# Sorted block attention and a residual MLP on one core: crossbar turns for q, moved mixing slots, and a last tile in halves

## Chip, cores and metric

The kernel runs on one core of a Trainium2 chip. The metric is the device time in microseconds. The page gives the granted TensorE clock as 0.999 of full speed.

## The reference

Shapes: q, k and v are (4 batches, 8 heads, 768 rows, 64), sort_net is (4, 8, 8, 8), and the output is (4, 768, 512), all float32. The MLP has 512 channels and 2048 hidden units.

```python
P = sort_net                       # five rounds of exp, divided by row sums, then column sums
for _ in range(5):
    P = exp(P - max(P)); P = P / sum(P, -1); P = P / sum(P, -2)
k_sorted = einsum('bhij,bhjcd->bhicd', P, k_b)      # 8 blocks of 96 rows are mixed
v_sorted = einsum('bhij,bhjcd->bhicd', P, v_b)
attn = softmax(q_b @ k_sb.T / sqrt(64))             # block by block
x = attn @ v_sb                                     # then heads side by side: (4, 768, 512)
a1 = alpha1 * x + beta1
tok = einsum('ts,bsd->btd', w_tok, a1)              # the token layer
u = x + lam * tok
a2 = alpha2 * u + beta2
out = u + lam * (max(a2 @ w_ch1, 0) @ w_ch2)        # the channel layers
```

## The kernel before

**The skeleton.** The channel layers of the four batches are the frame on which everything else hangs. A batch b is done in two halves hf of 384 rows. For each half, `h_unit` (line 692) makes 16 tiles of the hidden layer: four matmuls of 384 columns each into a PSUM tile h_ps, then a ReLU on ScalarE into hTa or hTb. Then `ch_unit` (line 695) makes three output tiles of 128 rows, each as four parts of four matmuls of 512 columns with hT as the stationary operand. VectorE multiplies the output tile by lam, and GpSimd adds u (VectorE in the last half of the last batch). Two DMAs of SP, of 96 and 32 rows, write it out.

I write h(b,hf) and c(b,hf) for these two stages. A stage h has the places h0 to h15 and a stage c the places c0 to c11, each of them a point behind one tile or part. `put(b, hf, kind, n, ...)` (line 791) hangs other work on a place, and the main loop at the end (lines 859 to 868) runs it there. This is an order written out by hand. TensorE, VectorE, ScalarE and GpSimd keep it as written, since they are recorded through a class `Engine` (line 55; so nearly every operation has line 65 in the profile). DMAs that SP issues are not recorded through it. SP takes them one after the other in the order that the builder gives them.

**What hangs on the frame.** While batch p = b - 1 goes through its channel layers, batch b is prepared:

- `load_kv` and `load_q` (lines 191 and 184) are loads by GpSimd's DMA queue from float32 to f16. q arrives as qn, with rows on the partitions, in six DMAs. The next batch is asked for at c11 of c(p,0).
- `mix_matrix` (354) makes the mixing matrices bigV, bigM and bigP of a batch: one matmul (repv_ps) and six VectorE operations (sel, red, bigV, bigM, two of bigP). For batches 2 and 3 it hangs at c5 of c(b - 2, 1).
- `mix_v` (508) mixes v in three parts of two matmuls (mix_ps), each copied by VectorE. `bounce_v` writes the result to DRAM with two SP DMAs (vscr), and `back_v` reads it as Vs, in another layout, with a third. For batches 2 and 3 these are at h10, h11, h12; h12; and c0.
- `mix_k` (523) mixes k in three parts of eight matmuls (kmix_ps), each copied by four operations into kT. For batches 2 and 3: c0 and c6 on ScalarE, c3 on VectorE.
- `q_turn_late` (495) turns q: for each of four head pairs six transposes on TensorE into a PSUM tile qt_ps, and one copy into qT by VectorE or ScalarE. For batches 2 and 3: c1, c4, c7, c7.
- `score` (397) needs all of kT and qT. It makes eight scores of a batch; each is eight matmuls (sc_ps) and one exp (et). `pv` (460) multiplies by Vs (x_ps). VectorE then takes a reciprocal and a product (x) and, one pv later, two operations for a. For batches 2 and 3, the scores start at c8 and pv at c10 of c(p,0), and they go on through h(p,1). `tails` moves some rows of a and x with six copies by VectorE.
- `moe_tok` (650) is the token layer: 18 matmuls for three row tiles (tok_ps), then on VectorE toktmp and u in f16 for each tile, and u in float32 on GpSimd. `moe_cross` (660) turns the f16 u by three crossbar DMAs of SP (uT), and `moe_affine` (667) makes a2T, on which the next h stage works. For the first half of batch 1 tokens and turns are at c5 and a2T at c8 of c(0,1); for batches 2 and 3 they are at c3 and c7.

**Buffers.** PSUM tiles come from two pools: psA with two slots (scores, x, mix, kmix, repv) and psB with four, which go round (h, ch, tok, qt). The output tile ost has two buffers, qT and qn one each, kT two.

Of the kernel before, what the change touches and what calls it, by code (L numbers as in the profile page):

```python
# [7 lines left out]
FT = mybir.dt.float32  # L8
F16 = mybir.dt.float16
# [7 lines left out]
def kernel(  # L17
# [20 lines left out]
    nc = tc.nc  # L38
# [315 lines left out]
    def mix_matrix(b):  # L354
        mix_values(b, psa)
        big = att.tile([128, 2, H * NB], F16, name="bigM", tag="bigM", bufs=3)
        dve.tensor_tensor(
            big[:], bigV[b][:].rearrange("p h i -> p (h i)").unsqueeze(1).to_broadcast([128, 2, H * NB]),
            mth[:].unsqueeze(2).to_broadcast([128, 2, H * NB]), ALU.mult,
        )  # L360
        bigM[b] = big
        bgp = att.tile([128, 2, 2, H4, NB], F16, name="bigP", tag="bigP", bufs=3)
        for th in range(2):
            dve.tensor_tensor(
                bgp[:, :, th, :, :], bigV[b][:].rearrange("p (g a) i -> p a g i", a=2),
                mth[:, th:th + 1].unsqueeze(2).unsqueeze(3).to_broadcast([128, 2, H4, NB]), ALU.mult,
            )
        bigP[b] = bgp
# [121 lines left out]
    def tails(x, lo, hi, eng):  # L490
        flush()
        for a in range(3):
            eng(x[96:128, a:a + 4:3, lo:hi], x[32 * a:32 * a + 32, 6:8, lo:hi])

    def q_turn_late(b, g, eng):
        if g == 0:
            qT_of[b] = att.tile([128, H4, S], F16, name="qT", tag="qT", bufs=1)
        ps = psb([128, S], F16, "qt_ps")
        for kt in range(NT):
            pe.transpose(  # L500
                ps[:, kt * 128:(kt + 1) * 128],
                qn_of[b][:, kt, 2 * g:2 * g + 2, :].rearrange("p a d -> p (a d)"), ident16[:],
            )
        eng(qT_of[b][:, g, :], ps[:])
# [3 lines left out]
    def mix_v(b, n, eng):  # L508
        if n == 0:
            mixed[b] = att.tile([128, HB, D], F16, name="mixed", tag="mixed", bufs=1)  # L510
        ps = psa([128, 2, 512], FT, "mix_ps")
        raw = raw_of[(b, 1)][:].rearrange("p t d -> p (t d)")
        for m in range(2):
            pe.matmul(
                ps[:, m, :], bigM[b][:].rearrange("p a x -> p (a x)"),
                raw[:, n * 1024 + m * 512:n * 1024 + (m + 1) * 512], start=True, stop=True,
            )
        eng(
            mixed[b][:, n * 16:(n + 1) * 16, :].rearrange("p t d -> p (t d)"),
            ps[:].rearrange("p m f -> p (m f)"),  # L520
        )

    def mix_k(b, n, engs):
        if n == 0:
            kT_of[b] = att.tile([128, H4, NB, BLK], F16, name="kT", tag="kT", bufs=2)
        ps = psa([128, 8, 128], FT, "kmix_ps")
        raw = raw_of[(b, 0)]
        for tp in range(8):
            pe.matmul(
                ps[:, tp, :], raw[:, 16 * n + 2 * tp:16 * n + 2 * tp + 2, :].rearrange("p t d -> p (t d)"),  # L530
                bigP[b][:].rearrange("p a t g i -> p (a t g i)"), start=True, stop=True,
            )
        dst = kT_of[b][:].rearrange("p g i (th tp par) -> p th (g i) tp par", th=2, par=2)
        for par in range(2):
            for h2 in range(2):
                engs[2 * par + h2](
                    dst[h2 * 64:h2 * 64 + 64, :, :, 8 * n:8 * n + 8, par],
                    ps[par * 64:par * 64 + 64, :, h2 * 64:h2 * 64 + 64].rearrange(
                        "p n (th c) -> p th c n", th=2
                    ),  # L540
                )

    def bounce_v(b):
        for th in range(2):
            nc.sync.dma_start(
                vscr[b, :, th * HB:(th + 1) * HB, :], mixed[b][th * 64:(th + 1) * 64, :, :],
            )
# [102 lines left out]
    def moe_tok(b, kt, ps):  # L650
        u32 = u_of[b]
        tok_part(b, kt, 0, C, ps)
        if b not in u16_of:
            u16_of[b] = moep.tile([128, NT, C], F16, name="u16", tag="u16", bufs=1)
        tmp = att.tile([128, C], FT, name="toktmp", tag="toktmp", bufs=2)
        dve.tensor_tensor(tmp[:], tok_of[(b, kt)][:], lamB[:], ALU.mult)
        dve.tensor_tensor(u16_of[b][:, kt, :], tmp[:], x_of[b][:, kt, :], ALU.add)
        (pool if b else dve).tensor_tensor(u32[kt], tmp[:], x_of[b][:, kt, :], ALU.add)
# [33 lines left out]
    def h_unit(b, hf, m):  # L692
        h_part(b, hf, m, range(CT))

    def ch_unit(b, hf, kk, part=(0, HT)):
        hT = hT_of[(b, hf)]
        kt = 3 * hf + kk
        if part[0] == 0:
            ch_of[0] = psb([128, C], FT, "ch_ps")
        cps = ch_of[0]  # L700
        for m in range(*part):
            pe.matmul(
                cps[:], hT[m][:, kk * 128:(kk + 1) * 128], W2p[:, m, :],
                start=(m == 0), stop=(m == HT - 1),
            )
        if part[1] < HT:
            return
        ost = att.tile([128, C], FT, name="ost", tag="ost", bufs=2)
        dve.tensor_tensor(ost[:], cps[:], lamB[:], ALU.mult)
        (dve if b == B - 1 and hf == 1 else pool).tensor_tensor(ost[:], ost[:], u_of[b][kt], ALU.add)  # L710
        act_out(out[b, kt * 96:(kt + 1) * 96, :], ost[0:96, :])
        act_out(out[b, TAIL + kt * 32:TAIL + (kt + 1) * 32, :], ost[96:128, :])
# [78 lines left out]
    def put(b, hf, kind, n, *todo):  # L791
        at.setdefault((b, hf, kind, n), []).extend(todo)
# [7 lines left out]
    for ks in range(NT):  # L800
        put(0, 0, "h", ks, lambda ks=ks: prep_wtok(ks, 1, psb, (dve.tensor_copy, act.copy)[ks % 2]))
    for n in range(1, B):
        put(max(n - 2, 0), n > 1, *(("h", 10), ("c", 5))[n > 1], lambda n=n: mix_matrix(n))
    put(0, 0, "h", 9, lambda: moe_cross(0, 1))
    for g in range(CT):
        put(0, 0, "h", g, lambda g=g: first_affine(0, slice(0, 128), slice(0, NT), slice(g * 128, (g + 1) * 128)))
# [3 lines left out]
    for b in range(1, B):  # L810
        p = b - 1
        off = 3 if b == 1 else 0
        for n in range(3):
            put(p, 0, "h", (13 if b == 1 else 10) + n, lambda b=b, n=n: mix_v(b, n, dve.tensor_copy))
        put(p, 0, "h", 15 if b == 1 else 12, lambda b=b: bounce_v(b))
        put(p, 0, "c", 4 if b == 1 else 0, lambda b=b: back_v(b))
        for n in range(3):
            put(p, 0, "c", off + 3 * n, lambda b=b, n=n: mix_k(b, n, ((act.copy, dve.tensor_copy)[n % 2],) * 4))
        for g in range(H4):
            put(p, 0, "c", off + (1, 4, 7, 7)[g], lambda b=b, g=g: q_turn_late(b, g, (dve.tensor_copy, act.copy, dve.tensor_copy, act.copy)[g]))  # L820
        if b + 1 < B:
            put(p, 0, "c", 11, lambda b=b: load_kv(b + 1), lambda b=b: load_q(b + 1))
        seq = [("s", 0), ("s", 1), ("s", 2), ("p", 0), ("s", 3), ("p", 1), ("p", 2), ("s", 4), ("p", 3), ("s", 5),
               ("p", 4), ("s", 6), ("p", 5), ("s", 7), ("p", 6), ("p", 7)]
        if b == 1:
            when = [("h", 0), ("h", 1), ("h", 2), ("h", 3), ("h", 4), ("h", 5), ("h", 6), ("h", 7), ("h", 8), ("h", 9),
                    ("h", 10), ("h", 11), ("h", 12), ("h", 13), ("h", 14), ("h", 15)]
        else:
            when = [("c", 8), ("c", 9), ("c", 10), ("c", 10), ("c", 11), ("c", 11), ("h", 0), ("h", 1), ("h", 2), ("h", 3),
                    ("h", 4), ("h", 5), ("h", 6), ("h", 8), ("h", 9), ("h", 11)]  # L830
        for (kind, n), (ph, at_) in zip(seq, when):
            f = (lambda b=b, n=n: score(b, n // 2, n % 2, psa)) if kind == "s" else (lambda b=b, n=n: pv(b, n // 2, n % 2))
            put(p, 1 if ph == "h" else 0, ph, at_, f)
        last = [("h", 12), ("h", 15)][b == 1]
        put(
            p, 1, *last, lambda b=b: tails(a1_of[b], 0, C, dve.tensor_copy),
            lambda b=b: tails(x_of[b], 0, C, dve.tensor_copy),
        )
        put(p, 1, "h", 4, lambda b=b: moe_start(b))
        for kt in range(3):  # L840
            put(p, 1, "c", 5 if b == 1 else 3, lambda b=b, kt=kt: moe_tok(b, kt, psb))
        put(p, 1, "c", 5 if b == 1 else 3, lambda b=b: moe_cross(b, 0))
        put(p, 1, "c", 8 if b == 1 else 7, lambda b=b: moe_affine(b, 0))
        for kt in range(3):
            put(b, 0, "h", 2 * kt, lambda b=b, kt=kt: moe_tok(b, 3 + kt, psb))
        put(b, 0, "h", 4, lambda b=b: moe_cross(b, 1))
        put(b, 0, "h", 13, lambda b=b: moe_affine(b, 1))
# [51 lines left out]
```

## Time and profile before

| | us |
|---|---|
| median of 7 runs | 277.2 |
| lowest, highest | 276.68, 279.44 |
| the profiled execution | 276.64 |
| its span in the trace | 274.9 |
| TensorE busy | 261.8 |
| VectorE, ScalarE, GpSimd busy | 166.5, 126.0, 97.3 |
| c(1,0) in the trace | 120.15 to 135.90 |
| h(1,1) | 135.90 to 150.10 |
| c(1,1) | 150.10 to 164.57 |
| h(2,0) | 164.57 to 180.15 |
| c(2,0) | 180.15 to 195.90 |

Times of a profile are from the start of its span. PE is TensorE, PEld its weight loads, DVE VectorE, ACT ScalarE, POOL GpSimd, SP SyncE; SPq is SP's queue of DMA issues. A row of the timeline has the start, the duration, the engine, the line, the operation with output and inputs, the number of instructions merged, and in brackets how long the engine had been idle before, with what ended that. Matmuls overlap in the pipeline, so the time from the start of one row to the start of the next is what TensorE spends; the duration of a row holds the latency of its last matmul too. A row of the table of stretches has the stretch, its length, then busy time and instruction count of PE, PEld, DVE, ACT and POOL, then the granted clock, the busy share of the DMA engines and GB/s.

### The profile page before, as it was taken

How to read it: one execution, taken by the hardware profiler on the slowest of the kernel's cores; microseconds unless marked ns; L12 is line 12 of the kernel's file. 1: busy time of each engine (PE TensorE's matmuls, PEld its weight loads, DVE VectorE, ACT ScalarE, POOL GpSimd, SP SyncE). 2: the span in 40 equal slices, each digit the busy share in tenths (PEclk: the TensorE clock that was granted, in tenths of full speed). 3: DMA queues.
4: the chain of work that ended last, by engine and by line, in shares of the span. 5: the costliest groups of instructions: out<-in, count | busy, mean ns of one | idle time of the engine just before them, and what ended most of it. 6: DMA issues, size and time to landing. Idle time of an engine off the chain costs nothing.

```text
span 274.9 us, 5418 instructions
## 1 busy us (share of the span) xinstructions
PE 261.8 (95%) x2205; PEld 141.3 (51%) x2205; DVE 166.5 (61%) x345; ACT 126.0 (46%) x231; POOL 97.3 (35%) x104
## 2 busy tenths in 40 slices
PE   7998999999999998999999999999999999999992
PEld 3466655445555444555455445555465445545540
DVE  5787517987378985466498784555679755121042
ACT  2588557225886002565777003566774004605600
POOL 8647103601571184402282556203100746032000
PEclk9999999999999999999999999999999999999999
DMA  6999999999999333249479932159300223012012
GB/s 105 215 202 191 206 208 214 176 114 185 126 180 170 24 95 97 40 99 119 89 149 182 91 86 70 38 118 127 102 4 2 76 57 79 19 38 76 2 38 76
DMA packets 60684, 29.46 MB, mean 107 GB/s; under 512 B 50082, under 2 KB 56242, under 8 KB 60660
## 3 DMA queue, kind: packets, MB, share of 16 engines
q0 software_dynamic: 26352, 15.34, 40.0%
q1 hardware_dynamic: 34308, 13.79, 26.3%
q8 instruction: 17, 0.28, 0.4%
q14 instruction: 7, 0.06, 0.1%
HBM read 32.79 MB, written 8.65 MB: 151 GB/s over the span
## 4 chain that ended last, share of the span: by engine, by line
PE 82%; DVE 8%; ACT 4%; DMA 3%; issue 2%; DVEq 0%; ACTq 0%; POOLq 0%
PE h_ps L65 29%; PE ch_ps L65 25%; PE tok_ps L65 10%; PE x_ps L65 3%; PE sc_ps L65 3%; ACT kT L65 2%; DVE x L65 2%; DVE a L65 2%; PE warm_ps L65 2%; DMA q<-in_q_dram 2%; PE kmix_ps L65 1%; PE mix_ps L65 1%; PE v_ps L65 1%; DVE ost L65 1%; PE qt_ps L65 1%
## 5 line engine op out<-in xcount | busy, mean ns | idle before, releaser
L65 PE MATMUL h_ps<-a2T,W1p 128*128 128x384 bf16 x512 | 95.9, 326 | 1.9 <-DVE a2T L65 1.5
L65 ACT ACTIVATE hTa<-h_ps 128x384 bf16<-128x384 f32 x96 | 47.0, 493 | 90.6 <-PE h_ps L65 90.4
L65 PE MATMUL ch_ps<-W2p,hTa 128*128 128x512 bf16 x288 | 68.4, 379 | 0.0
L65 POOL TENSOR_TENSOR ost<-ost,u 128x512 f32<-128x512 f32 x21 | 26.6, 1267 | 113.7 <-DVE ost L65 108.6
L65 PEld LDWEIGHTS <-W1p 128*128 128x128 bf16 x512 | 47.3, 98 | 33.5 <-issue 2.5
L65 PEld LDWEIGHTS <-hTa 128*128 128x128 bf16 x288 | 27.2, 98 | 29.0
L65 DVE TENSOR_TENSOR ost<-ch_ps,lamB 128x512 f32<-128x512 f32 x24 | 16.6, 691 | 39.7 <-PE ch_ps L65 36.8
L65 POOL TENSOR_TENSOR u<-toktmp,x 128x512 f32<-128x512 f32 x18 | 29.3, 1643 | 8.9 <-DVE toktmp L65 8.9
L65 PE MATMUL tok_ps<-a,w_tokT 128*128 128x512 f16 x126 | 29.7, 379 | 0.0
L65 ACT ACTIVATE et<-sc_ps 96x768 f16<-96x768 f32 (+1 forms) x32 | 25.6, 811 | 2.6 <-PE sc_ps L65 2.6
L65 PE MATMUL ch_ps<-W2p,hTb 128*128 128x512 bf16 x96 | 24.6, 379 | 0.0
L65 DVE TENSOR_TENSOR toktmp<-tok_ps,lamB 128x512 f32<-128x512 f32 x21 | 14.4, 688 | 13.3 <-PE tok_ps L65 12.0
L65 ACT CAST kT<-kmix_ps 64x512 f16<-64x512 f32 x24 | 17.1, 714 | 10.0 <-PE kmix_ps L65 9.7
L65 ACT ACTIVATE hTb<-h_ps 128x384 bf16<-128x384 f32 x32 | 15.7, 491 | 9.7 <-PE h_ps L65 9.5
L65 PEld LDWEIGHTS <-w_tokT 128*128 128x128 f16 x126 | 12.2, 98 | 13.8 <-DVE a L65 0.4
L65 DVE TENSOR_TENSOR u<-toktmp,x 128x512 f16<-128x512 f32 (+1 forms) x24 | 17.8, 750 | 0.7
L65 POOL DMA_DIRECT2D qn<-in_q_dram x18 | 16.0, 918 | 5.8 <-DMA raw<-in_v_dram 5.8
L65 DVE TENSOR_TENSOR x<-x_ps,rcb 96x512 f16<-96x512 f32 x24 | 16.5, 687 | 0.8
L65 PE MATMUL x_ps<-Vs,et 96*128 96x65 f16 (+4 forms) x288 | 14.4, 195 | 2.0 <-DVE x L65 1.0
L65 PEld LDWEIGHTS <-et 96*128 96x128 f16 (+4 forms) x288 | 12.5, 100 | 6.9 <-DVE x L65 2.2
L65 DVE TENSOR_SCALAR a2T<-uT,ab2col 128x384 bf16<-128x384 f16 x28 | 11.3, 461 | 5.0 <-DMA uT<-u 5.0
L65 DVE RECIPROCAL rcb<-x_ps 96x8 f32<-96x8 f32 x24 | 4.8, 200 | 15.5 <-PE x_ps L65 15.4
(113 smaller groups left out, 255.5 us busy)
## 6 DMA issues: line engine op xcount, KB each, us to landing
out_dram<-ost SPq DMA_DIRECT2D x24, 192.0 KB, 2.4
raw<-in_v_dram POOLq DMA_DIRECT2D x6, 384.0 KB, 8.6
raw<-in_k_dram POOLq DMA_DIRECT2D x6, 384.0 KB, 9.9
qn<-in_q_dram POOLq DMA_DIRECT2D x18, 128.0 KB, 10.1
vscr<-mixed SPq DMA_DIRECT2D x6, 384.0 KB, 4.0
Vs<-vscr SPq DMA_DIRECT2D x3, 768.0 KB
W1p<-in_moe_w_ch_dram POOLq DMA_DIRECT2D x4, 512.0 KB, 13.2
W2p<-in_moe_w_ch_dram POOLq DMA_DIRECT2D x4, 512.0 KB, 17.4
```

The lines of the kernel that those rows point to most:

```text
L65: ins = getattr(self.eng, name)(*args, **kwargs)
```

## The change

q of batches 2 and 3 is turned by six crossbar DMAs of SP at h11 of h(b - 1, 0) in place of 24 transposes on TensorE and four copies. For these batches mix_v goes from h10-h12 to h8-h10, the bounce from h12 to h10, and mix_k from c0, c3, c6 to h15, c1, c4, with the engines of its copies exchanged. mix_matrix of batches 2 and 3 goes from c5 to c9. Tokens and turns of batch 1's first half go from c5 to c4. The last output tile is made in two halves of 256 columns. Each half has a PSUM tile, 16 matmuls, two VectorE operations and two DMAs of its own, and the DMA for the last 32 rows is issued by ScalarE's queue.

```diff
+    def q_cross(b, kt):
+        if kt == 0:
+            qT_of[b] = att.tile([128, H4, S], F16, name="qT", tag="qT", bufs=1)
+        nc.sync.dma_start_transpose(
+            qT_of[b][:, :, kt * 128:(kt + 1) * 128], qn_of[b][:, kt, :, :].rearrange("p h d -> p (h d)"),
+        )
...
+    def last_out(hT, cps, kk, kt):
+        for n in range(2):
+            c = slice(n * C // 2, (n + 1) * C // 2)
+            if n:
+                cps = psb([128, C // 2], FT, "ch_ps")
+                for m in range(HT):
+                    pe.matmul(
+                        cps[:], hT[m][:, kk * 128:(kk + 1) * 128], W2p[:, m, c],
+                        start=(m == 0), stop=(m == HT - 1),
+                    )
+            ost = att.tile([128, C // 2], FT, name="ost", tag="ost", bufs=2)
+            dve.tensor_tensor(ost[:], cps[:, 0:C // 2], lamB[:, c], ALU.mult)
+            dve.tensor_tensor(ost[:], ost[:], u_of[B - 1][kt][:, c], ALU.add)
+            nc.sync.dma_start(out[B - 1, kt * 96:(kt + 1) * 96, c], ost[0:96, :])
+            nc.scalar.dma_start(out[B - 1, TAIL + kt * 32:TAIL + (kt + 1) * 32, c], ost[96:128, :])
...
+        w = C // 2 if b == B - 1 and kt == NT - 1 else C
...
-                cps[:], hT[m][:, kk * 128:(kk + 1) * 128], W2p[:, m, :],
+                cps[:, 0:w], hT[m][:, kk * 128:(kk + 1) * 128], W2p[:, m, 0:w],
...
+        if b == B - 1 and kt == NT - 1:
+            return last_out(hT, cps, kk, kt)
...
-        put(max(n - 2, 0), n > 1, *(("h", 10), ("c", 5))[n > 1], lambda n=n: mix_matrix(n))
+        put(max(n - 2, 0), n > 1, *(("h", 10), ("c", 9))[n > 1], lambda n=n: mix_matrix(n))
...
-            put(p, 0, "h", (13 if b == 1 else 10) + n, lambda b=b, n=n: mix_v(b, n, dve.tensor_copy))
-        put(p, 0, "h", 15 if b == 1 else 12, lambda b=b: bounce_v(b))
+            put(p, 0, "h", (13 if b == 1 else 8) + n, lambda b=b, n=n: mix_v(b, n, dve.tensor_copy))
+        put(p, 0, "h", 15 if b == 1 else 10, lambda b=b: bounce_v(b))
...
-            put(p, 0, "c", off + 3 * n, lambda b=b, n=n: mix_k(b, n, ((act.copy, dve.tensor_copy)[n % 2],) * 4))
-        for g in range(H4):
+            put(
+                p, 0, *(("c", 3 + 3 * n) if b == 1 else (("h", 15), ("c", 1), ("c", 4))[n]),
+                lambda b=b, n=n: mix_k(b, n, ((act.copy, dve.tensor_copy)[(n + (b > 1)) % 2],) * 4),
+            )
+        for kt in range(NT if b > 1 else 0):
+            put(p, 0, "h", 11, lambda b=b, kt=kt: q_cross(b, kt))
+        for g in range(0 if b > 1 else H4):
...
-            put(p, 1, "c", 5 if b == 1 else 3, lambda b=b, kt=kt: moe_tok(b, kt, psb))
-        put(p, 1, "c", 5 if b == 1 else 3, lambda b=b: moe_cross(b, 0))
+            put(p, 1, "c", 4 if b == 1 else 3, lambda b=b, kt=kt: moe_tok(b, kt, psb))
+        put(p, 1, "c", 4 if b == 1 else 3, lambda b=b: moe_cross(b, 0))
```

In the order that the builder gives SP, the six q turns of batch 2 come behind the outputs of c(0,0), and those of batch 3 behind the outputs of c(1,0). Behind each six come the first output pair of the next c stage and the three uT turns for the first half of the batch before (batch 1 and batch 2).

## The prediction

> **What bounds the kernel now.** I read the page's busy rows first, then the chain that ended last, then the timeline wherever TensorE was not simply streaming.
>
> ```profile
> PE 261.8 (95%) x2205; PEld 141.3 (51%) x2205; DVE 166.5 (61%) x345; ACT 126.0 (46%) x231; POOL 97.3 (35%) x104
> ...
> PE 82%; DVE 8%; ACT 4%; DMA 3%; issue 2%; DVEq 0%; ACTq 0%; POOLq 0%
> ```
>
> TensorE is the bound: busy 95%, 82% of the chain, clock 0.999. Two things shorten the kernel: work taken off TensorE, and its few waits. The table of stretches gives stage c(1,0) and its twin c(2,0), 15.75 us each:
>
> ```profile
> 120.15:135.90 15.75, 15.29 (x145) 8.44 (x144) 7.16 (x14) 10.29 (x16) 2.54 (x2) 1.00 0.88 134
> ...
> 180.15:195.90 15.75, 15.30 (x146) 8.43 (x144) 7.16 (x14) 10.30 (x16) 2.54 (x2) 1.00 0.89 134
> ```
>
> The timeline inside c(1,0) shows q's transposes between output matmuls, and a wait:
>
> ```profile
> 122.32 0.50 PE L65 MATMUL qt_ps<-ident,qn 128*128 128x128 f16 x6
> 122.66 1.03 PE L65 MATMUL ch_ps<-W2p,hTa 128*128 128x512 bf16 x4
> ...
> 128.40 2.91 ACT L65 CAST kT<-kmix_ps 64x512 f16<-64x512 f32 x4 [1.37 <-PE kmix_ps L65]
> ...
> 129.73 1.03 PE L65 MATMUL ch_ps<-W2p,hTa 128*128 128x512 bf16 x4
> ...
> 131.36 0.34 PE L65 MATMUL sc_ps<-qT,kT 64*128 64x96 f16 x7 [0.46 <-ACT kT L65]
> ...
> 131.64 1.04 PE L65 MATMUL ch_ps<-W2p,hTa 128*128 128x512 bf16 x4
> ...
> 132.88 1.04 PE L65 MATMUL ch_ps<-W2p,hTa 128*128 128x512 bf16 x4
> ```
>
> Six transposes hold TensorE for 122.66 - 122.32 = 0.34 us. The first score waits for the last k copies: from one output slot to the next it is 1.91 us (129.73 to 131.64), where the same work without a wait takes 1.24 (131.64 to 132.88), so 0.67 is lost. The sum closes: 12 output slots at 0.864, 3 k mixings at 0.45, 4 q groups at 0.34, 4 scores at 0.38, 2 p at 0.28 and 0.67 make 15.83, against 15.75.
>
> The largest other wait opens h(1,0):
>
> ```profile
> 98.14 4.29 SPq L663 DMA_TRANSPOSE uT<-u  x3
> ...
> 103.65 1.35 DVE L65 TENSOR_SCALAR a2T<-uT,ab2col 128x384 bf16<-128x384 f16 x4 [1.84 <-DMA uT<-u]
> ...
> 104.08 1.30 PE L65 MATMUL h_ps<-a2T,W1p 128*128 128x384 bf16 x4 [1.54 <-DVE a2T L65]
> ```
>
> The last output slot started at 101.52, so h could have started at 102.38 and the token matmuls after it at 103.03; the timeline has those at 105.22. 2.2 us are lost, behind a crossbar turn (2.29 us in the chain) that waited for VectorE's u rows (last at 101.20).
>
> **q by crossbar.** Gone from the path: 2 batches x 4 groups x 0.34 = 2.7 us of TensorE. The 8 copies of qT (0.55 us VectorE, 0.80 ScalarE) go too, off the path. The nearest row for what is added is the same instruction on the same shape (128 x 512, f16): 21 uT turns, 1197 ns of SP each, 2.3 us to landing, 3.9 at worst. The Trainium skill speaks against it: "VectorE: DVE Perf Modes", "The three transpose paths" and "Rules for kernel authors", puts a 128x128 transpose at 390 ns on TensorE and 1309 by the crossbar, and takes TensorE when PSUM will do. By those prices 48 transposes lose 44 us if serial. The rows here differ in kind: TensorE's pipelined cost is 57 ns, and one turn of four blocks holds SP, not TensorE. What decides is whether anybody waits for SP.
>
> SP is FIFO, and the built order puts the six q turns of a batch just ahead of an output pair and the three uT turns of the batch before. Batch 2: they need the last score of batch 1 (86 us) and qn, whose packets end about 92; six at 1.2 end about 93.5, and the output pair behind them is ready at 96.1. Free. Batch 3: qn's packets end about 155.5 (DMA view), so the sixth ends about 157.1, the output pair 157.9, and three uT turns 161.5 instead of 161.26. h(2,0) has 0.5 us of slack there. But the turns share the DMA engines with the loads they wait for (share 0.95 in 135.9 to 150.1); each uT turn keeps them full for about 0.75 us, so three could put qn back 2 us and TensorE wait 2.0. Bounds 0 to 2.0; I take 0.5, near the undisturbed end, since the loads are thinning (555 packets in 153-154, 125 in 154-155).
>
> **k and v mixing, batches 2 and 3.** Same matmuls, earlier. v at h8-h10: copies end about 1.3 us earlier relative to the stage. From the bounce (119.75, 179.75) to Vs's last packet took 11.8 and 12.4 us; bounced 2.2 us before c starts, Vs is there 9.5 to 10.2 after; p0 wants it at 11.5. k at h15, c1, c4 by VectorE, ScalarE, VectorE: the last copies (2.90 us) run 5.3 to 8.2 us into c, and the first score comes at 8.7. So the 0.67 goes, twice, with 0.5 us to spare; if VectorE is late it returns. Gain 1.3 us, bounds 0 and 1.4 (nothing more was waited for).
>
> **Token layer of batch 1 at c4, matrix of batch 2 at c9.** Before, the matrix work (sel to bigP, 94.63 to 96.66) held VectorE 2.0 us ahead of the u rows. Now u ends about 99.5 and uT lands about 101.8. TensorE reaches the tokens at 92.2, before the tail copies end (92.68): 0.2 lost. The four a2T end about 103.3, so the token matmuls start about 103.5, not 105.22: 1.7 gained. The matrix work now follows a2T: 103.3 to 105.3, with the output multiply behind it to 106.0. PSUM slots go round in four, so the third h group waits for that multiply: it wants to start at 105.5, and loses 0.5. Net gain 1.2, bounds 0.3 and 2.2. For batch 3 the matrix moves from c5 to c9; its multiply ends about 166.9, where the third group wants 167.0: nothing, covered by 0.1 us; uncovered it is within the crossbar's term.
>
> **Last tile in halves.** TensorE: the split adds nothing by pitch (512 columns 0.216, 384 0.162, 128 0.056 us, so 256 should take 0.109; 32 make 3.5 against 3.46). The skill's "TensorE: Matmul & The Clock Gate", "Back-to-back issue gap", also gives a sustained 131 ns for 512 and 81 for 128; by that, halves near 95 would add 0.9 us. The 216 here excludes it. At the end:
>
> ```profile
> 268.00 0.32 SPq L711 DMA_DIRECT2D out_dram<-ost  x1
> 268.36 0.42 SPq L712 DMA_DIRECT2D out_dram<-ost  x1
> ...
> 269.95 0.69 DVE L65 TENSOR_TENSOR ost<-ch_ps,lamB 128x512 f32<-128x512 f32 x1 [1.98 <-PE ch_ps L65]
> 270.67 0.69 DVE L65 TENSOR_TENSOR ost<-ost,u 128x512 f32<-128x512 f32 x1
> ```
>
> A half costs VectorE about 0.42 (between 0.21 at 64 columns and 0.69 at 512), so two steps take 0.83, not 1.4, and ScalarE's queue spares the second issue (0.37). That would be 1.0. But ost has two buffers: the second half takes the one of the tile before, whose output started at 268.36 and lands 2.2 later, 270.6. So it waits 0.65 us after TensorE: gain 0.3. ScalarE issues no DMA before; SP's 0.42 is the nearest row. Bounds -0.3 and 1.0.
>
> **Sum.** 2.7 + 1.3 + 1.2 + 0.3 - 0.5 = 5.0, less 0.1 for the narrow k cover: 4.9. The profiled execution took 276.64 us, span 274.9 and 1.7 around it; it becomes 271.7. The seven runs' median is 277.2, 0.56 above that execution, so the forecast is 277.2 - 4.9 = 272.3. Ends: all good, 2.7 + 1.4 + 2.2 + 1.0 = 7.3, 269.9; all bad, 2.7 + 0 + 0.3 - 0.3 - 2.0 = 0.7, 276.5, not all together.
>
> **Rivals.** *Late transfers take the wait's place*: Vs or the uT turns of batch 2 come 1 to 2 us late, or k's cover fails. For it: SP's outputs queue behind Vs (issues of 3.2 and 4.8 us), DMA share 0.88. Against: the margins above. Time 277.2 - 4.9 + 2.2 = 274.5. Chance 0.24. *The crossbar is serial under load* (the slower side): each q turn waits for the last to land. Place: SP ahead of uT. At 2.3 us, batch 2's six end at 99.9, delaying uT by 3; batch 3's, from about 151, end at 164.8, delaying it by 7.7. TensorE waits about 2.6 + 7.2, so 277.2 - 4.9 + 9.8 = 282. It decides from about 1.8 us each. Against: three uT turns took 3.91 us of SP under full DMA load at 55.6, 1.3 each. Chance 0.07. *The two buffer waits and the q turns cost nothing*: 277.2 - 4.9 - 0.5 - 0.65 - 0.5 = 270.7, chance 0.12. The forecast itself, 271.3 to 273.3: 0.57.
>
> About 0.5% (1.4 us) is what a measurement can tell from no change. Faster 0.87, same 0.06 (the worst of the late transfers), slower 0.07. The 8-in-10 range is 269.9 to 275.2.
>
> **What would show it.** After: c(1,0) and c(2,0) about 13.3 us, h's longer by 0.45, no qt_ps rows; no kT wait before the first score; the h(1,0) wait about 0.5 plus 0.5 for the slot; six q turns in about 7 us with uT behind them undelayed; the last multiply waiting for a DMA. I am wrong if x_ps waits for Vs, if uT in h(2,0) comes over 1 us late, or if the q turns take 2 us each.

## The result and the profile after

The changed kernel takes 275.61 us (median of 24 runs, 272.97 to 276.83), the kernel before 277.14 beside it (59 runs). The ratio, which is one of means, is 0.9916, 95% interval [0.9898, 0.9934]: about 2.3 us faster. The medians lie 1.5 us apart; 4.9 were forecast. One thing must be known to read these numbers: in 13 of the 24 runs TensorE's mean granted clock is 0.994 or less, and these have the median 276.03, where the other 11, called undisturbed below, have 273.95; the experiments show why. The profiled execution took 275.79 us, span 274.0, at a mean clock of 0.999.

The page first, its busy row and the shares of its chain:

```profile
PE 260.3 (95%) x2173; PEld 140.3 (51%) x2173; DVE 170.1 (62%) x351; ACT 117.3 (43%) x219; POOL 96.3 (35%) x104
...
PE 77%; DMA 7%; SPq 5%; DVE 3%; issue 3%; POOL 1%; ACT 1%; POOLq 0%; DVEq 0%
```

TensorE lost its transposes and is still the bound. SP's queue, which had no share of the chain before, now has 5%, and DMA 7% where it had 3%: something that sets the end now passes through SP. By lines, q's turns have 3% of it and the load of qn, which they wait for, 4%.

The table of stretches, at c(1,0) and c(2,0):

```profile
121.05:134.18 13.13, 13.13 (x112) 6.48 (x111) 8.34 (x13) 5.51 (x9) 2.53 (x2) 1.00 0.93 139
...
182.20:195.36 13.16, 13.16 (x113) 6.48 (x111) 8.33 (x13) 5.52 (x9) 2.53 (x2) 1.00 0.95 139
```

13.1 us each, with TensorE busy in all of it; about 13.3 was announced. From here on, rows of a timeline that do not bear on the reading are left out. The timeline where the kT wait was:

```profile
126.29 2.91 DVE L65 CAST kT<-kmix_ps 64x512 f16<-64x512 f32 x4 [0.62 <-PE kmix_ps L65]
...
129.64 0.34 PE L65 MATMUL sc_ps<-qT,kT 64*128 64x96 f16 x8
129.92 1.04 PE L65 MATMUL ch_ps<-W2p,hTa 128*128 128x512 bf16 x4
```

The last k copy ends at 129.20, 0.44 us ahead of the first score, which has no bracket any more: nothing is waited for. The start of h(1,0) in the timeline:

```profile
104.04 1.25 DVE L65 TENSOR_SCALAR a2T<-uT,ab2col 128x384 bf16<-128x384 f16 x4 [1.84 <-DMA uT<-u]
104.47 1.19 PE L65 MATMUL h_ps<-a2T,W1p 128*128 128x384 bf16 x4
105.51 1.46 PE L65 MATMUL tok_ps<-a,w_tokT 128*128 128x512 f16 x6
```

TensorE's row has no bracket any more, where its wait was 1.54 us. The times look later than before (103.65, 105.22), but the whole execution was: c(0,0) starts at 61.03 here and at 59.18 there, and the code up to it is the same. So I compare shifts, not times. Where a stage begins in both traces, the difference changes only by what happened in between:

| TensorE at | before | after | shift | gained since the row above |
|---|---|---|---|---|
| start of c(0,0) | 59.18 | 61.03 | +1.85 | -1.85 |
| token matmuls of h(1,0) | 105.22 | 105.51 | +0.29 | 1.56 |
| end of c(1,0) | 135.90 | 134.18 | -1.72 | 2.01 |
| token matmuls of h(2,0) | 165.22 | 166.69 | +1.47 | -3.19 |
| end of c(2,0) | 195.90 | 195.36 | -0.54 | 2.01 |
| end of the span | 274.9 | 274.0 | -0.9 | 0.35 |

The 1.85 us of the prologue are chance in this one execution: ScalarE's fourth a2T comes at 42.24 here, at 40.39 before, and at 40.33 to 40.94 in the other ten profiles of this case, whose prologue is the same; two of them are of the changed kernel itself. Every gain is there. What is not in the forecast's size is the row of -3.19. The timeline there, first before:

```profile
157.44 3.82 SPq L663 DMA_TRANSPOSE uT<-u  x3
...
162.55 1.85 DVE L65 TENSOR_SCALAR a2T<-uT,ab2col 128x384 bf16<-128x384 f16 x4 [0.53 <-DMA uT<-u]
...
165.22 1.46 PE L65 MATMUL tok_ps<-a,w_tokT 128*128 128x512 f16 x6
```

Then after:

```profile
149.53 8.21 SPq L498 DMA_TRANSPOSE qT<-qn  x6
...
157.83 0.53 SPq L737 DMA_DIRECT2D out_dram<-ost  x1
158.41 1.76 SPq L738 DMA_DIRECT2D out_dram<-ost  x1
...
160.27 3.82 SPq L670 DMA_TRANSPOSE uT<-u  x3
...
161.99 1.03 PE L65 MATMUL ch_ps<-W2p,hTb 128*128 128x512 bf16 x4
...
165.22 1.25 DVE L65 TENSOR_SCALAR a2T<-uT,ab2col 128x384 bf16<-128x384 f16 x4 [5.16 <-DMA uT<-u]
165.66 1.19 PE L65 MATMUL h_ps<-a2T,W1p 128*128 128x384 bf16 x4 [2.63 <-DVE a2T L65]
...
166.69 1.46 PE L65 MATMUL tok_ps<-a,w_tokT 128*128 128x512 f16 x6
```

Read the second from the bottom. TensorE stands 2.63 us for a2T, which stands for the crossbar turn uT. uT's three turns begin at 160.27, where before they began at 157.44 although the rest of the kernel is now 1.72 us earlier: 4.55 us later in the kernel's own terms. Ahead of them SP had six q turns, 8.21 us, and an output pair, 2.3 us. The last tile:

```profile
267.82 0.42 SPq L738 DMA_DIRECT2D out_dram<-ost  x1
...
269.93 0.42 DVE L65 TENSOR_TENSOR ost<-ch_ps,lamB 128x256 f32<-128x256 f32 x1 [1.35 <-DMA out_dram<-ost]
270.39 0.43 DVE L65 TENSOR_TENSOR ost<-ost,u 128x256 f32<-128x256 f32 x1
```

The last multiply now waits for a DMA, the output of the tile before, as announced.

### The profile page after: what moved, and what is told of

Its sections match the earlier page's. It is cut to its first block, busy times and chain, and to the rows that moved or that the text cites. A ratio compares the mean times of both kernels' runs of the same rounds, so it can differ in the third digit from the quotient of the medians.

```text
span 274.0 us, 5380 instructions
## 1 busy us (share of the span) xinstructions
PE 260.3 (95%) x2173; PEld 140.3 (51%) x2173; DVE 170.1 (62%) x351; ACT 117.3 (43%) x219; POOL 96.3 (35%) x104
## 4 chain that ended last, share of the span: by engine, by line
PE 77%; DMA 7%; SPq 5%; DVE 3%; issue 3%; POOL 1%; ACT 1%; POOLq 0%; DVEq 0%
PE h_ps L65 27%; PE ch_ps L65 23%; PE tok_ps L65 10%; DMA qn<-in_q_dram 4%; PE warm_ps L65 4%; SPq L498 3%; PE x_ps L65 3%; PE sc_ps L65 2%; DMA out_dram<-ost 2%; PE mix_ps L65 1%; PE v_ps L65 1%; DVE ost L65 1%; PE kmix_ps L65 1%; SPq L737 1%; SPq L670 1%
## 5 line engine op out<-in xcount | busy, mean ns | idle before, releaser
L65 PE MATMUL ch_ps<-W2p,hTa 128*128 128x512 bf16 (+1 forms) x300 | 68.5, 371 | 0.0
L65 PEld LDWEIGHTS <-hTa 128*128 128x128 bf16 x300 | 28.4, 98 | 29.0
L65 DVE TENSOR_TENSOR ost<-ch_ps,lamB 128x512 f32<-128x512 f32 (+1 forms) x25 | 16.7, 669 | 37.8 <-PE ch_ps L65 34.6
L65 PE MATMUL ch_ps<-W2p,hTb 128*128 128x512 bf16 (+1 forms) x100 | 24.8, 371 | 0.0
L65 DVE TENSOR_TENSOR u<-toktmp,x 128x512 f16<-128x512 f32 (+1 forms) x24 | 19.5, 824 | 0.7
L65 DVE CAST kT<-kmix_ps 64x512 f16<-64x512 f32 x20 | 14.2, 709 | 4.5 <-PE kmix_ps L65 3.0
L65 DVE TENSOR_SCALAR a2T<-uT,ab2col 128x384 bf16<-128x384 f16 x28 | 10.5, 439 | 9.8 <-DMA uT<-u 9.8
L65 ACT CAST kT<-kmix_ps 64x512 f16<-64x512 f32 x16 | 11.4, 715 | 9.8 <-PE kmix_ps L65 9.6
```

The costliest lines, as they stand in the source:

```text
L65: ins = getattr(self.eng, name)(*args, **kwargs)
```

## The experiments

Theory A: the loss is the FIFO of SP in h(2,0), where uT queues behind q's turns. Rivals: B, the DMA engines under the loads, or VectorE late with the matrix work, rather than the queue's order; C, late Vs or k copies, or lost gains elsewhere; and, from the split of the 24 runs, D: the wait in h(2,0) makes the chip lower TensorE's clock, so that the wait costs more than its own length. Ratios are to the kernel before on the same chip; its median was 277.14 beside the first four, 277.21 beside the next four, 276.95 at the last two.

**e1: q of batch 3 back on TensorE.** Of the changed kernel, two lines:

```diff
-        for kt in range(NT if b > 1 else 0):
+        for kt in range(NT if b == 2 else 0):
...
-        for g in range(0 if b > 1 else H4):
+        for g in range(0 if b == 2 else H4):
```

> The changed kernel with q of batch 3 turned on TensorE again (24 transposes and four copies at the old places); q of batch 2 stays on the crossbar. Theory A (the six q turns of batch 3 stand on SP's queue ahead of the uT turns that h(2,0) waits for): the 3.2 us lost at the start of h(2,0) go, 1.36 us of TensorE work come back in c(2,0), so the time is about 1.8 us under the changed kernel's, near 273.8, and uT in h(2,0) starts within 0.5 us of its u rows. Theory B (the start of h(2,0) is late because the matrix work of batch 3 or VectorE is late there): the wait stays, and the time is 1.4 us above the changed kernel's, near 277.0.

Measured 272.48 us (272.03 to 272.64, 5 runs), ratio 0.9817 [0.978, 0.9854]. Its timeline at h(2,0):

```profile
154.11 4.42 SPq L670 DMA_TRANSPOSE uT<-u  x3
159.75 1.32 DVE L65 TENSOR_SCALAR a2T<-uT,ab2col 128x384 bf16<-128x384 f16 x4 [1.06 <-DMA uT<-u]
160.62 1.03 PE L65 MATMUL ch_ps<-W2p,hTb 128*128 128x512 bf16 x4
161.49 0.81 PE L65 MATMUL h_ps<-a2T,W1p 128*128 128x384 bf16 x4
```

h follows ch 0.87 us later, its streaming time, with no bracket. Putting 1.36 us of transposes back on TensorE made the kernel 3.1 us faster. It is better even than A asked for. All five runs have a clock of 0.996 or more, and from the undisturbed 273.95 the sum comes near: 273.95 - 3.2 + 1.36 = 272.1. The loads and the matrix work are where the changed kernel has them, so neither alone makes uT late.

**e2: q's turns a stage earlier, in a fixed order.** All turns are issued through an `Engine` of SP, which keeps them in the order written, and q's are hung on h0 of h(b - 1, 0):

```diff
+    turns = Engine(nc.sync)
...
-        nc.sync.dma_start_transpose(
+        turns.dma_start_transpose(
...
-            put(p, 0, "h", 11, lambda b=b, kt=kt: q_cross(b, kt))
+            put(p, 0, "h", 0, lambda b=b, kt=kt: q_cross(b, kt))
```

The second of these edits stands twice, for q's turns and for uT's.

> The changed kernel with all crossbar turns kept in the written order on SP's queue, and the q turns hung at h0 of h(b-1,0), so that they come behind the uT turns of h's own half. Nothing else changes. Theory A: h(2,0) starts without the 3.2 us wait, c(1,0) and c(2,0) stay at 13.3 us, and the time is near 275.6 - 3.2 = 272.4 or a little less. Theory B: the wait in h(2,0) stays at about 2.6 us and the time stays near 275.6. Theory C (crossbar turns slow other transfers wherever they are): the wait moves to the start of the other uT turns or to Vs, and x_ps or a2T waits for a DMA in h(2,0) or c(2,0).

Measured 277.39 us (275.98 to 281.43, 22 runs), ratio 0.9992 [0.9969, 1.0016]: the whole gain is gone. At h(2,0) A held: h_ps follows the last ch_ps without a wait. But the turns now hold SP at 108.23 to 116.7 and at 168.48 to 176.2. The timeline behind the first of these, batch 2's:

```profile
116.76 3.84 SPq L65 DMA_TRANSPOSE uT<-u  x3
120.69 1.18 SPq L553 DMA_DIRECT2D vscr<-mixed  x2
121.88 1.25 DVE L65 TENSOR_SCALAR a2T<-uT,ab2col 128x384 bf16<-128x384 f16 x4 [4.48 <-DMA uT<-u]
...
125.96 0.62 PE L65 MATMUL kmix_ps<-bigP,raw 128*128 128x128 f16 x8 [1.46 <-DVE kT L65]
```

One late queue delays four things: uT of the second half, v's bounce behind it, a2T, for which VectorE stands 4.48 us, and k's copies behind a2T on VectorE, for which TensorE waits. In c(2,0) the late bounce costs more: x_ps waits 2.03 us for Vs. So the wait had only moved, which is C's mechanism with A's cause. 12 of the 22 runs have a clock of 0.994 or less, down to 0.98, so part of the spread may be D's; the other ten still have the median 276.3. The eight microseconds of SP need a place where nothing behind them is urgent.

**e3: the v and k slots alone**, on the kernel before (h8-h10 and h10 for v, h15, c1, c4 for k, nothing else).

> The kernel before with only the new slots for v and k mixing of batches 2 and 3 (q stays on TensorE at c1, c4, c7, c7). By the step of the prediction the kT wait of 0.67 us goes in c(1,0) and in c(2,0): 1.3 us less than before, near 275.8. Rival: VectorE is late with the last k copies, or the q copies collide with them, and the wait stays: no change, 277.1.

Measured 275.56 us (275.31 to 277.24, 13 runs), ratio 0.9936 [0.9912, 0.996]. The gain of about 1.6 us is the two kT waits of 0.67, and a little more. C falls for this part: TensorE has no wait for Vs or kT in this trace.

**e4: the token slots alone**, on the kernel before (tokens of batch 1 at c4, mix_matrix of batches 2 and 3 at c9).

> The kernel before with only the token layer and turns of batch 1 at c4 and the mixing matrices of batches 2 and 3 at c9. By the step of the prediction h(1,0) starts 1.2 to 1.6 us earlier and nothing else moves: near 275.7. Rival: the late matrix work holds the output multiply, so that the third group of h(1,0) or of h(2,0) waits for its PSUM slot and half or more of the gain is given back: above 276.4.

Measured 275.46 us (275.32 to 276.38, 8 runs), ratio 0.9935 [0.9911, 0.9959]: a gain of about 1.7, against 1.56 in the table. The rival, half of it given back, falls.

**e5: work put into the wait.** Twelve dummy matmuls on zeros, 2.6 us, at the end of c(1,1) of the changed kernel; uT is as late as before. Theory A alone sees no use in it, D does:

```diff
+    put(1, 1, "c", 11, lambda: warm(12))
```

> The changed kernel with 12 idle matmuls of 512 columns on zeros (2.6 us at 0.216) behind c11 of c(1,1), where TensorE waits for the late uT turns. The wait itself stays as long. Theory D (the wait of over 2.6 us makes the chip now and then halve TensorE's clock for a while, which costs some runs 2 us): the runs with a mean clock of 0.994 or less, 13 of 24 in the changed kernel, become rare, the median falls to about 274.1 and the spread shrinks, though nothing was taken away. Rival (the low clock is chance, or comes from elsewhere): the share of such runs stays near a half and the median near 275.6, or 0.2 higher for the added work.

Measured 274.43 us (274.14 to 275.13, 6 runs), ratio 0.9899 [0.9878, 0.992]. The timeline has the filling and the same DMA wait of VectorE:

```profile
160.99 2.75 PE L65 MATMUL warm_ps<-wz 128*128 128x512 f16 x12
163.13 1.25 DVE L65 TENSOR_SCALAR a2T<-uT,ab2col 128x384 bf16<-128x384 f16 x4 [4.93 <-DMA uT<-u]
163.58 1.17 PE L65 MATMUL h_ps<-a2T,W1p 128*128 128x384 bf16 x4
```

Useless work made the kernel 1.2 us faster than the changed one, and no run of the six has a low clock. D holds. The time stays 0.5 us above the undisturbed 273.95; this trace has a wait of 0.76 us for Vs in c(2,0), which the changed kernel's does not have.

**e9: the changed kernel, two more executions**, for a trace of the low clock.

> The changed kernel once more, one look. Theory D: a run of 275.3 us or more has a stretch with a low granted clock right behind the wait at the start of h(2,0) (163 to 170 us), and a run of about 274 has none there. Rival: the low clock lies elsewhere, at a place that has nothing to do with the change.

> The changed kernel a third time, one look, with the same expectation: a low granted clock right behind the wait at the start of h(2,0) in a run of 275.3 us or more, none there in a run of about 274.

Both executions (275.71 and 275.29 us, mean clock 0.994 and 0.993) show it. The first one's table of stretches behind the wait; the third column from the end is the granted clock:

```profile
163.00:165.00 2.00, 1.13 (x5) 0.48 (x5) 1.52 (x6) 0.00 (x0) 0.00 (x0) 1.00 0.45 131
165.00:166.00 1.00, 1.00 (x5) 0.34 (x4) 0.93 (x6) 0.49 (x1) 0.00 (x0) 0.73 0.00 0
166.00:167.00 1.00, 1.00 (x4) 0.39 (x3) 0.54 (x1) 0.00 (x0) 0.33 (x1) 0.50 0.00 0
167.00:168.00 1.00, 1.00 (x5) 0.48 (x4) 0.75 (x2) 0.00 (x0) 0.95 (x2) 0.50 0.00 0
168.00:169.00 1.00, 1.00 (x5) 0.44 (x4) 0.63 (x1) 0.49 (x1) 1.00 (x1) 0.56 0.23 63
169.00:170.00 1.00, 1.00 (x7) 0.49 (x5) 0.00 (x0) 0.49 (x1) 0.64 (x1) 1.00 0.68 199
```

and its timeline:

```profile
163.87 1.19 PE L65 MATMUL h_ps<-a2T,W1p 128*128 128x384 bf16 x4 [2.32 <-DVE a2T L65]
164.91 2.20 PE L65 MATMUL tok_ps<-a,w_tokT 128*128 128x512 f16 x6
166.90 2.44 PE L65 MATMUL h_ps<-a2T,W1p 128*128 128x384 bf16 x8
169.18 1.46 PE L65 MATMUL tok_ps<-a,w_tokT 128*128 128x512 f16 x6
```

After a wait of 2.32 us TensorE starts at full speed, and about 1.6 us later the clock goes to 0.50 for some 3.4 us. Six token matmuls and eight of h take 1.99 and 2.28 us to the next row, where they take 1.30 each at full clock: 1.67 us lost. The second execution has the low clock at another point (the last line is from its timeline):

```profile
163.00:165.00 2.00, 1.16 (x4) 0.50 (x4) 1.56 (x6) 0.00 (x0) 0.00 (x0) 0.72 0.45 131
165.00:166.00 1.00, 1.00 (x4) 0.40 (x3) 0.93 (x6) 0.49 (x1) 0.00 (x0) 0.50 0.00 0
166.00:167.00 1.00, 1.00 (x4) 0.36 (x3) 0.50 (x1) 0.00 (x0) 0.37 (x1) 0.50 0.00 0
167.00:168.00 1.00, 1.00 (x6) 0.49 (x5) 0.26 (x1) 0.00 (x0) 0.90 (x1) 0.85 0.00 0
...
163.84 1.42 PE L65 MATMUL h_ps<-a2T,W1p 128*128 128x384 bf16 x4 [2.34 <-DVE a2T L65]
```

A mean of 0.72 over the first 2 us means that 1.1 of them were at 0.50, so the clock fell at about 163.9, with the restart at 163.84, and it rose again at 167.3: 3.4 us as in the first. The same matmuls lose about 1.3 us there. The gap between the medians of the two groups of runs is 2.1, more than either loss; the rest is not explained.

The Trainium skill, "TensorE: Matmul & The Clock Gate", "What's actually happening", has a rule near it: idle for at least one window of about 3.4 us halves the clock, and the window runs freely. By its length no row here would be enough. The measurement says otherwise: behind rows of 2.32 and 2.34 us the clock was halved, and behind the one of 2.63 us in the first profile it was not. So the length of the wait alone does not decide it. That the low clock hits only some runs, and not at a fixed time from the restart, would suit a window that is not tied to the kernel, but no run here shows the window itself.

**e6: q's turns right behind the uT turns.** Ordered as in e2, and hung on the place of the uT turns, one stage ahead of where the change has them:

```diff
-            put(p, 0, "h", 11, lambda b=b, kt=kt: q_cross(b, kt))
+            put(p - 1, 1, "c", 4, lambda b=b, kt=kt: q_cross(b, kt))
```

> The changed kernel with the crossbar turns kept in the written order on SP's queue, and the q turns hung right behind the uT turns of c(b-2,1), so that they hold SP between 161 and 168.5 us, where only outputs wait behind them. Theory A: the 3.2 us at the start of h(2,0) go, nothing else waits: 277.14 - 1.6 - 2 x 2.0 - 0.35 = 271.2. Theory C (crossbar turns delay what stands near them wherever they are): uT of the second halves or the output buffers are late instead, and the time stays above 273.

Measured 271.06 us (270.72 to 271.86, 5 runs), ratio 0.9782 [0.9758, 0.9806], with no low clock. The timeline at h(2,0):

```profile
158.38 7.76 SPq L65 DMA_TRANSPOSE qT<-qn  x6
159.50 1.25 DVE L65 TENSOR_SCALAR a2T<-uT,ab2col 128x384 bf16<-128x384 f16 x4 [1.35 <-DMA uT<-u]
160.08 1.03 PE L65 MATMUL ch_ps<-W2p,hTb 128*128 128x512 bf16 x4
160.94 0.81 PE L65 MATMUL h_ps<-a2T,W1p 128*128 128x384 bf16 x4
```

The same six turns, no cheaper (7.76 us), now follow uT and hold up nothing: h comes 0.86 us after ch. What was left of B falls too: beside these six no load runs, and they take 1.3 us each all the same. In the changed kernel one turn starts every 1.3 us from 151.3 to 156.5, though its loads end by 154; only the second turn came about 0.5 us late, as for its input. Against e1, which keeps batch 3's q on TensorE, the crossbar is worth 1.4 us for that batch by the medians, the 4 x 0.34 of the prediction.

**e7: the last half's output in another buffer**, on e6:

```diff
-            ost = att.tile([128, C // 2], FT, name="ost", tag="ost", bufs=2)
+            ost = att.tile([128, C // 2], FT, name="ost", tag=("ost", "toktmp")[n], bufs=2)
```

> The same, with the last half tile in a buffer of its own (the free one of toktmp) in place of the second ost buffer. If the last multiply waits for the output DMA of the tile before, as the prediction has it, 0.5 to 0.7 us go: 270.6. Rival: the last output DMA ends the kernel in any case at the same time: no change.

Measured 270.85 us (270.57 to 271.13, 5 runs), ratio 0.9763 [0.9743, 0.9783], the fastest of all. The row of the last multiply in its timeline:

```profile
264.71 0.43 DVE L65 TENSOR_TENSOR ost<-ch_ps,lamB 128x256 f32<-128x256 f32 x1 [0.86 <-PE ch_ps L65]
```

The releaser is TensorE and no longer the DMA of the tile before; the idle time fell from 1.36 us in e6 to 0.86. The 0.5 us are shown in the trace. In the medians it is 0.2, which these intervals cannot tell apart.

**e8: the kernel before, with its wait in h(1,0) filled** by nine dummy matmuls. It asks whether the wait of 2.2 us that the change shortens had a part in the same effect. The 37 runs that the expectation counts hold 11 with the low clock, not 10.

> The kernel before with 9 idle matmuls of 512 columns (1.9 us) behind c11 of c(0,1), in its wait of 2.2 us for uT. Theory D: the runs with a mean clock of 0.994 or less, 10 of 37 in the kernel before, and their 278.5 us and more go; the median stays near 276.95. Rival: they stay at about a quarter.

Measured 276.96 us (276.61 to 277.79, 14 runs), ratio 0.9993 [0.9982, 1.0004]. The median hardly moves. No run of these 14 has a clock of 0.994 or less, where 13 of 56 runs of the kernel before have. e4, which shortens the same wait by moving the tokens, has none in 8 runs; e3, which leaves it, has 2 in 13. None in 22, where 13 of 56 would give five, is hardly chance and points to the same mechanism. But no trace of the kernel before shows where its clock falls: this stays open.

## Why the prediction was right and wrong

The direction and all four gains were right; the price was not.

- *q's transposes and the kT wait.* 1.36 + 0.67 = 2.03 us in each of two stages was the sum; each gained 2.01. VectorE's narrow cover for the k copies held by 0.44 us.
- *Token slots.* Net 1.2 was taken; 1.56 came. That is the 1.7 gained, nearly, and the 0.5 lost to the PSUM slot did not come. I had given the matrix work the 2.0 us it took before; in its new place it took 1.25, because bigV takes 0.23 us there and 1.01 before.
- *Last tile.* 0.3 was taken, 0.35 came, and the wait for the second ost buffer stood where it was put: 0.65 us was taken for it, and e7 takes 0.5 of the row's 1.36 away.
- *The failed step* is the one on SP in "q by crossbar": "Batch 3: qn's packets end about 155.5 (DMA view), so the sixth ends about 157.1, the output pair 157.9, and three uT turns 161.5 instead of 161.26", from which I took 0.5 with bounds 0 and 2.0. It cost 3.19. The last landing plus one turn is the end of six turns only when the loads are slower than the turns. They were not: SP began with the first landing, at 149.53, and needed 8.21 us for six. In the times before that is 151.25 + 8.21 = 159.5, not 157.1, and already 2.4 us too late. The output pair behind them took 2.3 us and not 0.75 (1.4 in the same place before). So uT's turns began 4.55 us later in the kernel's own terms. a2T ended 3.79 us later (164.40 before, 166.47 after, with the 1.72), mostly since its four operations took 1.25 us there and not 1.85; 0.6 of that was slack, and 3.19 reached TensorE, more than the upper bound.
- *What stood against it in the prediction.* The numbers were in the text: the serial rival counts six turns "from about 151", at 2.3 us each. At the row's own 1.3 they would have ended at 158.8, against the forecast's 157.1. I computed the same queue in two ways and kept the kinder one. For batch 2 the same step put the end of the six at 93.5; they ended at 96.78, which is 94.9 in the times before. That this cost nothing was luck: the output pair behind them was ready only at 96.1. The rival "Late transfers take the wait's place" named the right victim, batch 2's uT, and gave it 2.2 us and a chance of 0.24.
- *What no step had*: a wait of TensorE can cost more than its length. It put 1.7 us on the median (273.95 in the undisturbed runs, 275.61 in all).

The undisturbed runs close the sum: 277.14 - 1.6 - 2 x 2.01 - 0.35 + 3.2 = 274.4, measured 273.95; from 276.94, the median of the 26 undisturbed runs of the kernel before beside the first four experiments, it is 274.2. With both costs gone it is 277.14 - 1.6 - 4.0 - 0.35 = 271.2, and e6 measured 271.06.

What stays open: whether the kernel before loses some of its runs to its own wait in h(1,0) (e8), and why the prologue of the one profiled execution was 1.85 us late.

## What to carry to other kernels

For work moved to a DMA queue, add up the queue: it starts when its first input lands and takes the number of issues times the time of each, and everything behind it waits for all of it; then put it behind the last urgent issue, which here was worth 4.5 us (e6 against the change) at the same work. Fix the order of such a queue by hand when the order decides. A wait of TensorE as long as the 2.3 to 2.6 us here is better shortened or filled, since behind it the clock was halved in some runs.

## What the runs showed of the hardware that was not expected

- Six crossbar turns of 128 x 512 f16, one behind the other, hold SP's queue for 7.75 to 8.52 us in these traces, about 1.3 to 1.4 each. A plain output issue behind them took 1.76 us instead of 0.42; before, with no q turns ahead of it, it took 1.11.
- TensorE's clock fell to 0.50 for 3.4 us after idle rows of 2.3 us, in one trace 1.6 us behind the restart and in the other at the restart; behind a row of 2.6 us in a third it did not fall. The mean clock of 13 of 24 runs agrees with one such drop (1.7 of 274 us is 0.6%). Filling the wait with matmuls on zeros took it away, in 6 of 6 runs.
- bigV, a VectorE product of 128 x 64 elements, takes 1.01 us in one place and 0.23 in another; GpSimd's work was beside it in the first. That this is the cause was not tried.
